# A gated mix of two attention paths: two second feature differences and two low weight parts on POOL in place of VectorE

## The chip, the core and the metric

The kernel runs on one core of a Trainium2 chip. The metric is the device time of one execution in microseconds (us). Five engines work side by side, each through its own queue in order: TensorE (PE in the profile; its weight loads are listed as PEld), VectorE (DVE), ScalarE (ACT), GpSimd (POOL) and SyncE (SP), whose queue in this kernel issues the DMA transfers. They wait for each other through semaphores.

## What is computed

Two attention paths read the same input x of 2048 tokens by 448 features, with 16 heads of 28 features each, and a gate per token mixes them.

```python
def _A_ref(x, wqkv, w_phi, wo):
    qkv = (x @ wqkv) -> q, k, v per head
    pq = jnp.einsum("bhsd,hdf->bhsf", q, w_phi)
    pk = jnp.einsum("bhsd,hdf->bhsf", k, w_phi)
    phi_q = jnp.concatenate([_softmax(pq, axis=-1), _softmax(-pq, axis=-1)], axis=-1)
    phi_k = jnp.concatenate([_softmax(pk, axis=-1), _softmax(-pk, axis=-1)], axis=-1)
    kv = jnp.einsum("bhsf,bhsd->bhfd", phi_k, v)
    z  = jnp.einsum("bhsf->bhf", phi_k)
    num = jnp.einsum("bhqf,bhfd->bhqd", phi_q, kv)
    den = jnp.einsum("bhqf,bhf->bhq", phi_q, z)[..., None] + 1e-6
    return (num / den) -> all heads side by side @ wo

g = _sigmoid((x * gate_w).sum(-1, keepdims=True))
a = _A_ref(x, A_wqkv, A_w_phi, A_wo)
b = softmax attention of x with B_wqkv, B_wo
return g * a + (1 - g) * b
```

Path A is a linear attention whose features are two softmaxes, one of the projected values and one of their negatives. Path B is an ordinary softmax attention over all 2048 keys.

## The kernel before

**Numbers.** Operands of the large matmuls are split in two parts: a high part, which is a copy in TensorE's rounded format, and a low part, the difference between the raw value and the high part. A product then takes three passes (high by high, high by low, low by high). `split_weight` (lines 141 to 144) makes both for a weight: ScalarE copies the high part at once, and the subtraction for the low part is put into a list, `lows`, which `take_lows` (line 137) empties later in the program.

**Stages.** First come the projections of path B's queries and keys, then a loop over i from 0 to 42 (line 694). Its first 16 turns treat path A's key tiles of 128 tokens, turns 16 to 31 the query tiles, with q = i - 16 the number of the tile, and the rest drains what is under way. After that path B's scores, exponentials and value products fill the larger part of the time. Between these, `mx_unit` (line 238) works through the maxima of path B's scores: four small matmuls (pmd and pmb, line 260), two Relu activations (line 264) and two VectorE operations with a running maximum (line 265).

**One query tile in the loop.** In the order of the program text, turn q does this:

1. PE projects the tile into the PSUM tile `pq` (line 729).
2. `features1` (line 420): ScalarE copies pq to SBUF (`pc`, line 423). VectorE reduces the largest and the smallest value of each head (`ext`, lines 425 and 426). POOL subtracts the largest value (the first difference, line 431). The second difference, smallest value minus pc (line 433), is made by the engine that the caller passes. The exponential over both (line 436) is put into the list `exps`.
3. From q = 8 on, and in a few earlier turns, one `mx_unit`.
4. In every second turn from q = 7 on, `normalize2` (line 387) for an earlier pair of tiles: VectorE adds a constant to the denominators `dena` and takes the reciprocal (lines 390 and 391); SyncE stores them to DRAM (`rda`, line 395) and reads them back broadcast to 128 partitions (`rsa`, line 396).
5. From q = 10 on, in every second turn, `normalize4` (line 405): ScalarE makes the high part of a normalized pair and POOL the low part (`oTa`, lines 410 and 411).
6. The exponential of the tile before, q - 1 (line 436, ScalarE).
7. `features2` (line 439) for tile q - 1: VectorE sums (line 443) and takes the reciprocal (line 444), POOL multiplies (line 445).
8. In every second turn from q = 9 on, `normalize3` (line 400): VectorE multiplies a pair by the broadcast `rsa` (line 402).
9. `take_lows` (line 761), then, in turns 4 and 6, `split_part` for a half of woA (lines 770 and 771). Since `take_lows` stands ahead of it, the two low parts of woA come in turns 5 and 7.
10. `numer` in every second turn (line 513): PE makes numerators and denominators (`pn`), ScalarE copies them out (`oUa`, line 381), SyncE moves the denominators (`dena`, line 384).
11. `turn` (line 497): PE transposes the features of an earlier tile (`pft`, line 507), ScalarE copies them (`fT`, line 510).
12. From q = 11 on, `out_a` (line 527): PE multiplies `oTa` by woA, high and low part (`poa`); ScalarE scales by the gate (`ga`, line 535) and SyncE stores it (`gad`).

**PSUM.** pq, pn, pft and poa share four PSUM banks (lines 63 and 718), so a new one waits until the one four places earlier has been copied out by ScalarE. The matmuls of `mx_unit` have four banks of their own.

**Order.** The order of PE, VectorE, ScalarE and POOL is that of the program text (`manual_schedule`, lines 52 to 54). SyncE is not in that list: the order of its transfers is set by the framework when the program is built.

**Staging.** Raw weights of the query stage lie in a pool of two buffers (`stg`, line 713). woA arrives in both (`part_loads`, line 767). The raw weights of path B's values, `wvB`, are loaded into the same two buffers (line 769), each after the low part of woA has been taken from it.

The lines that the change touches stand in this loop: line 735, which names the engine of the second difference for each query tile, and line 771, which splits woA.

Of the kernel before, what the change touches and what calls it, by code (L numbers as in the profile page):

```python
# [19 lines left out]
D = 448  # L20
# [21 lines left out]
def gated_mix_kernel(ctx, tc, xT, wqkB, wvB, wvA, wkAT, wqAT, phi, woA, woB,  # L42
# [7 lines left out]
    nc = tc.nc  # L50
# [90 lines left out]
    def split_weight(w, raw, bs, cs, low=nc.vector, high=nc.scalar.copy):  # L141

        high(w[:, 0, bs, cs], raw)
        lows.append(lambda: low.tensor_sub(w[:, 1, bs, cs], raw, f32(w[:, 0, bs, cs])))
# [20 lines left out]
    def take_acts():  # L165
        while acts:
            acts.pop(0)()

    def take_subs():
        while subs:  # L170
            subs.pop(0)()
# [66 lines left out]
    def mx_unit():  # L238

        u = mxs["u"]  # L240
        if u == NF:
            return
        mx_fin()
        mxs["u"] = u + 1
        gq, r = divmod(u, 16)
        g, qb = divmod(gq, NQ)
        c, qt = divmod(r, 4)
        hp, b = divmod(c, 2)
        col = 64 * gq + 16 * b + 4 * qt + 2 * hp
        if r in (4, 9) and gq + 1 < GM:  # L250
            pair_query(gq + 1, r // 9)
        if r == 4 and gq + 1 == GM:
            mx_query(GM)
        qc, kc = mxs[("qp", gq, hp)], mxs[("kp", g, c)]

        pm = [ps_mx(f"pm{'ddbb'[j]}{u}_{j % 2}") for j in range(4)]
        for j in range(4):
            i = (j + 2) % 4
            js = slice(32 * i, 32 * i + DH)
            nc.tensor.matmul(pm[j], qc[js, qt * P:(qt + 1) * P], kc[js, :], start=True, stop=True,  # L260
                             tile_position=(32 * i, 0))
        for i in range(2):
            rl = rlp.tile([P, 512], F32, tag="rl", name=f"rl{u}_{i}", bufs=psn[2])
            nc.scalar.activation(rl, pm[i], AF.Relu)  # L264
            nc.vector.tensor_tensor_reduce(rl, pm[2 + i], rl, 1.0, LOWEST, ALU.add, ALU.max,  # L265
                                           part[:, col + i:col + i + 1])
        if gq + 1 < GM and qt == 3 and qb == NQ - 1:
            pair_load(g + 1, c)
        if gq + 1 == GM and qt == 3:
            mx_load(GM // NQ, c)  # L270
        if r == 15:
            mx_reduce(gq)
# [147 lines left out]
    def features1(pp, nm, eng):  # L420

        pc = bd.tile([P, H, DH], F32, tag="pc", name=f"pc{nm}", bufs=2)
        nc.scalar.copy(pc, pp[:, :D].rearrange("p (h f) -> p h f", f=DH))
        ext = bd.tile([P, 2, H], F32, tag="ext", name=f"ext{nm}", bufs=3)
        nc.vector.tensor_reduce(ext[:, 0, :], pc, AX.X, ALU.max)
        nc.vector.tensor_reduce(ext[:, 1, :], pc, AX.X, ALU.min)
        fw = bd.tile([P, H, 64], F32, tag="feat", name=f"feat{nm}", bufs=4)
        f = fw[:, :, :2 * DH].rearrange("p h (s f) -> p h s f", s=2)
        if nm in ("k0", "k1", "k2", "k3"):
            nc.gpsimd.memset(fw[:, :, 2 * DH:], 0.0)  # L430
        nc.gpsimd.tensor_sub(f[:, :, 0, :], pc,
                             ext[:, 0, :].unsqueeze(2).to_broadcast([P, H, DH]))
        eng.tensor_sub(f[:, :, 1, :],
                             ext[:, 1, :].unsqueeze(2).to_broadcast([P, H, DH]), pc)
        fe = fw[:, :, :2 * DH]
        exps.append(lambda: nc.scalar.activation(fe, fe, AF.Exp))
        return fw
# [12 lines left out]
    def take_exps(left=0):  # L450
        while len(exps) > left:
            exps.pop(0)()

    fk, va, fq, fT_of, num, oTs = {}, {}, {}, {}, {}, {}
# [26 lines left out]
    def kv_copy():  # L481

        kvT = ta.tile([P, D], F32, tag="ga", name="kvT", bufs=2)
        kvw = kvT[:, :256].rearrange("p (g f) -> p g f", f=64)
        nc.vector.memset(kvw[:, :, 56:], 0.0)
        nc.scalar.copy(kvw[:, :, :56],
                       pkv[:, :224].rearrange("p (g f) -> p g f", f=56))
        return kvT
# [93 lines left out]
    def split_part(w, key, n, i, low=nc.vector):  # L582
        split_weight(w, raws[key][i], slice(2 * i, 2 * i + 2), slice(0, n), low)
# [110 lines left out]
    for i in range(2 * NT + 11):  # L694
        t, q = i, i - NT
        y = q - 1
        tb = y // 2
        take_acts()
        if t < NT and t % 2 == 0:
            mx_unit()  # L700
            passes = (55 if t < NT - 4 else 44) + (4 if t >= 4 else 0)
            pace["n"], pace["at"] = 4 if t >= 4 else 0, [k * passes // 4 for k in range(1, 4)]
        if q in (0, 1):
            take_exps()

        if t % 2 == 0 and 0 <= t - 4 < NT:
            kv_add(t - 4)
            kv_add(t - 3)
        if q == 2:
            bk_s.close()  # L710
            ta_s = ExitStack()
            ta = ta_s.enter_context(tc.tile_pool(name="ta", bufs=1, reuse_waits="tile"))
            stg = ta_s.enter_context(tc.tile_pool(name="stg", bufs=2, reuse_waits="tile"))
            KV = ta.tile([P, 2, P], F32, name="KV")
            kvT = kv_copy()
            ps_s_.close()
            ps = ps_s_.enter_context(tc.tile_pool(name="psq", bufs=1, space=PSUM, reuse_waits="tile"))
            psn[0] = 4
            woA_s = weights(3, "woA_s")
            wvB_s = weights(2, "wvB_s")  # L720
            take_exps()
        if t < NT:
            pk = ps_s(f"pk{t}")
            tok_major(pk, t, wkA_s, D, tick)
            fk[t] = features1(pk, f"k{t}", nc.gpsimd)
            take_exps(1)
        if 0 <= q < NT:
            pq = ps_s(f"pq{q}")
            tok_major(pq, q, wqA_s, D)
        if q == 0:  # L730
            fk[NT - 1] = features2(fk[NT - 1], f"k{NT - 1}")
        if q in (1, 2):
            fq[q - 1] = features2(fq[q - 1], f"q{q - 1}")
        if 0 <= q < NT:
            fq[q] = features1(pq, f"q{q}", nc.vector if q in (1, 3, 4, 5, 6, 7, 8) else nc.gpsimd)
        if 0 <= t - 1 < NT - 1:
            fk[t - 1] = features2(fk[t - 1], f"k{t - 1}")
        if q in (0, 1) or q >= 8:
            mx_unit()
        if y >= 6 and y % 2 == 0 and tb - 3 < 8:  # L740
            num[tb - 3] = normalize2(ta, *num[tb - 3], f"a{tb - 3}", 2, True)
        if y >= 9 and y % 2 and tb - 4 < 8:
            oTs[tb - 4] = normalize4(ta, num.pop(tb - 4), f"a{tb - 4}", 2)
        if q > 0:
            take_exps(int(q < NT))
        if q == 3:
            kv_out(kvT)
        if 2 <= q - 1 < NT:
            fq[q - 1] = features2(fq[q - 1], f"q{q - 1}")
        take_subs()  # L750
        if t == 1:
            pair_load(0, 3)
        if y >= 8 and y % 2 == 0 and tb - 4 < 8:
            num[tb - 4] = normalize3(*num[tb - 4], 2)
        if t < NT:
            value_a(t)
            if t % 2 and t < NT - 4:
                proj_qk(NP + t // 2, ev)
        if q in (0, 1):
            proj_qk(NP + 6 + q, ev)  # L760
        take_lows()
        if 2 <= i < 6:
            fold(wqA_s, "q", i - 2)
        if q == 1:
            ev_s.close()
        if q == 2:
            part_loads("woA", woA, D, "woA")
        if q == 11:
            part_loads("wvB", wvB, D, "wvB")
        if q in (4, 6):  # L770
            split_part(woA_s, "woA", D, (q - 4) // 2)
        if q in (14, 17):
            split_part(wvB_s, "wvB", D, (q - 14) // 3)
        if q == 1:
            gates()
        if y >= 4 and y % 2 == 0 and tb - 2 < 8:
            numer(tb - 2)
        if y < 9 or y % 2:
            if y >= 2 and y - 2 < NT:
                turn(y - 2)  # L780
        if 0 <= y - 10 < NT:
            out_a(y - 10)
            out_a2(y - 10)
        if y >= 9 and y % 2 == 0 and y - 2 < NT:
            turn(y - 2)
        if NT + 3 <= q < NT + 10:
            mx_unit()
        if q == NT + 6:
            ps_s_.close()
            ps = ps_s_.enter_context(tc.tile_pool(name="psv", bufs=1, space=PSUM, reuse_waits="tile"))  # L790
            psn[:2] = 2, 6
        if q == NT + 2:
            bd_s.close()
            vb = [value_tile(0)]
        if 0 <= q - NT - 2 < 8:
            value_b(q - NT - 2)
# [434 lines left out]
```

## Time and profile before

| what | value |
|---|---|
| median of three runs | 985.07 us (985.03 to 985.94) |
| profiled execution, device time | 983.83 us |
| its span, first to last instruction | 982.0 us |
| mean granted TensorE clock | 0.998 of full |
| query stage, turns 0 to 15 | from about 186 us; the last tile's features near 263 us |
| the stretch that the change touches | about 203 to 222 us |

The profile shows one execution. Its page gives the busy time of each engine, a row of the costliest groups of instructions, and the chain of waits followed back from the last instruction. In a row of a group stand the line of the code, the engine, the operation, the tiles written and read, their size and type, the count, the busy time in us and the mean of one in ns, and then the idle time ahead of them with what ended it. Tiles of one name are counted together: featq is the feature tile of a query tile, oUa, oTa, rsa, rda and dena belong to path A's normalization, oUb, oTb, rsb and denb to path B's. A row of the timeline gives the start and the length in us; in brackets stands the idle time of the engine just before, and what ended it. In the chain of waits, "issue" is time in which an engine waited for nothing that the profile shows, and SPq is SyncE's queue.

### The profile page before, as it was taken

How to read it: one execution, taken by the hardware profiler on the slowest of the kernel's cores; microseconds unless marked ns; L12 is line 12 of the kernel's file. 1: busy time of each engine (PE TensorE's matmuls, PEld its weight loads, DVE VectorE, ACT ScalarE, POOL GpSimd, SP SyncE). 2: the span in 40 equal slices, each digit the busy share in tenths (PEclk: the TensorE clock that was granted, in tenths of full speed). 3: DMA queues.
4: the chain of work that ended last, by engine and by line, in shares of the span. 5: the costliest groups of instructions: out<-in, count | busy, mean ns of one | idle time of the engine just before them, and what ended most of it. 6: DMA issues, size and time to landing. Idle time of an engine off the chain costs nothing.

```text
span 982.0 us, 22542 instructions
## 1 busy us (share of the span) xinstructions
PE 973.6 (99%) x8510; PEld 602.8 (61%) x8510; DVE 724.1 (74%) x1335; ACT 752.3 (77%) x1442; POOL 235.9 (24%) x229
## 2 busy tenths in 40 slices
PE   9999999999999999999999999999999999999998
PEld 8877877776877664555555555555555555555555
DVE  5566767898765678888888888888888888885112
ACT  5455655577876688898898898898898898897662
POOL 1135535578744800031011011011011011010010
PEclk9999999999999999999999999999999999999999
DMA  9973010113233233121232121122231222100441
GB/s 307 311 255 113 33 54 32 40 26 92 76 108 120 89 118 123 41 58 41 67 89 69 41 62 41 61 79 68 70 83 41 65 62 65 41 21 31 141 151 57
DMA packets 56140, 84.49 MB, mean 86 GB/s; under 512 B 17216, under 2 KB 23984, under 8 KB 56032
## 3 DMA queue, kind: packets, MB, share of 16 engines
q1 hardware_dynamic: 56032, 83.06, 27.1%
q8 instruction: 67, 1.10, 0.5%
q14 instruction: 41, 0.34, 0.1%
HBM read 54.86 MB, written 27.78 MB: 84 GB/s over the span
## 4 chain that ended last, share of the span: by engine, by line
PE 91%; DVE 4%; DMA 2%; issue 1%; ACT 1%; POOL 0%; SPq 0%; DVEq 0%; POOLq 0%; ACTq 0%
PE g L850 29%; PE pv L995 27%; PE pqk L109 5%; PE pk L127 4%; PE pva L127 4%; PE g L288 3%; PE poa L109 3%; PE pob L109 3%; PE pmd L260 3%; PE pvb L127 2%; PE pvb L109 1%; PE pq L109 1%; PE pqk L621 1%; DMA rsa<-rda 1%; DMA gad<-ga 1%
## 5 line engine op out<-in xcount | busy, mean ns | idle before, releaser
L858 ACT ACTIVATE p<-g 128x512 f32<-128x512 f32 x1020 | 525.6, 609 | 82.8 <-PE g L850 82.6
L295 DVE TENSOR_REDUCE part<-g 128x1 f32<-128x512 f32 x704 | 442.4, 684 | 84.0 <-PE g L288 82.8
L850 PEld LDWEIGHTS g<-qst,kst 32*128 32x128 f32 x3060 | 221.2, 183 | 215.5 <-DVE part L295 194.8
L850 PE MATMUL g<-qst,kst 32*128 32x512 f32 x3060 | 338.0, 419 | 0.1
L995 PE MATMUL pv<-p,vb 128*32 128x512 f32 x2048 | 273.0, 605 | 0.0
L288 PE MATMUL g<-kc,qc 28*128 28x512 f32 x704 | 233.3, 495 | 0.0
L402 POOL TENSOR_TENSOR oUb<-oUb,rsb 128x512 f32<-128x512 f32 x15 | 19.3, 1288 | 491.5 <-DMA rsb<-rdb 369.2
L265 DVE CUSTOM_DVE_ANT_0 rl<-pmb,rl 128x512 f32<-128x512 f32 x160 | 103.3, 683 | 45.5 <-ACT rl L264 45.5
L264 ACT ACTIVATE rl<-pmd 128x512 f32<-128x512 f32 x160 | 87.4, 601 | 32.0 <-PE pmb L260 29.7
L288 PEld LDWEIGHTS g<-kc,qc 28*128 28x128 f32 x704 | 86.3, 181 | 0.2
L995 PEld LDWEIGHTS pv<-p,vb 128*32 128x32 f32 x2048 | 40.6, 108 | 66.0 <-issue 64.7
L109 PE MATMUL pqk<-XH,wB 128*128 128x512 f32 x192 | 59.1, 396 | 0.0
L260 PE MATMUL pmb<-kp,qp 28*128 28x512 f32 x160 | 43.2, 495 | 1.9 <-DVE part L265 1.1
L559 ACT CAST ev<-pqk 128x512 fp32r<-128x512 f32 x28 | 16.0, 589 | 37.8 <-PE pqk L109 21.5
L1006 DVE SCALAR_TENSOR_TENSOR acc<-pob,gate,acc 128x448 f32<-128x448 f32 x12 | 8.2, 684 | 48.3 <-PE pob L109 35.2
L109 PE MATMUL poa<-woA_s,oTa 128*128 128x448 f32 x192 | 43.7, 376 | 0.0
L109 PEld LDWEIGHTS pqk<-XH,wB 128*128 128x128 f32 x192 | 35.4, 188 | 8.5 <-issue 1.5
L560 DVE TENSOR_TENSOR ev<-pqk,ev 128x512 fp32r<-128x512 f32 x28 | 19.0, 690 | 29.3 <-ACT ev L559 29.2
L260 PE MATMUL pmd<-kp,qp 28*128 28x512 f32 x160 | 39.9, 494 | 0.0
L127 PE MATMUL pk<-wkA_s,XH 128*128 128x448 f32 x128 | 39.4, 382 | 0.0
L109 PEld LDWEIGHTS poa<-woA_s,oTa 128*128 128x128 f32 x192 | 34.9, 188 | 6.7 <-issue 3.0
L109 PE MATMUL pq<-wqA_s,XH 128*128 128x448 f32 x128 | 37.4, 374 | 0.6 <-ACT oUa L381 0.6
(156 smaller groups left out, 1073.3 us busy)
## 6 DMA issues: line engine op xcount, KB each, us to landing
qkd<-ev SPq DMA_DIRECT2D x28, 512.0 KB
qst<-qkd SPq DMA_DIRECT2D x64, 112.0 KB
kst<-qkd SPq DMA_DIRECT2D x64, 112.0 KB
od<-oTb SPq DMA_DIRECT2D x48, 112.0 KB
rsa<-rda SPq DMA_DIRECT2D x8, 512.0 KB
oL<-od SPq DMA_DIRECT2D x8, 512.0 KB
rsb<-rdb SPq DMA_DIRECT2D x15, 256.0 KB
gad<-ga SPq DMA_DIRECT2D x16, 224.0 KB
```

Of the source, the lines that this page charges most:

```text
L109: nc.tensor.matmul(dst, l, r, start=i == 0, stop=i == len(todo) - 1)
L127: nc.tensor.matmul(dst[:, :n], l, r, start=i == 0, stop=i == len(todo) - 1, skip_group_check=True)
L260: nc.tensor.matmul(pm[j], qc[js, qt * P:(qt + 1) * P], kc[js, :], start=True, stop=True, tile_position=(32 * i, 0))
L264: nc.scalar.activation(rl, pm[i], AF.Relu)
L265: nc.vector.tensor_tensor_reduce(rl, pm[2 + i], rl, 1.0, LOWEST, ALU.add, ALU.max, part[:, col + i:col + i + 1])
L288: nc.tensor.matmul(pm, mxs[("qc", gq)][js, qt * P:(qt + 1) * P], mxs[("kc", gq // NQ, kb)][js, :], start=True, stop=True, tile_position=(3 ...
L295: nc.vector.tensor_reduce(part[:, col:col + 1], pm, AX.X, ALU.max)
L402: (nc.gpsimd if n == 1 else nc.vector).tensor_mul(oU, oU, rs)
L560: nc.vector.tensor_sub(e[:, 1, :], pq, f32(e[:, 0, :]))
L850: nc.tensor.matmul(st[j], kst_of[(gq // NQ, kt // 4)][js, k, (kt % 4) * P:(kt % 4 + 1) * P], qst_of[gq][js, q, :], start=n == 0, stop=n == ...
L858: nc.scalar.activation(p, st[j], AF.Exp, scale=SCALE)
L995: nc.tensor.matmul(pv[32 * j:32 * j + 32, :], vb[kt // 8][:, kt % 8, 4 * g + j, :], pt[j], start=kt == 0, stop=kt == NT - 1, tile_position ...
```

## The change

```diff
         if 0 <= q < NT:
-            fq[q] = features1(pq, f"q{q}", nc.vector if q in (1, 3, 4, 5, 6, 7, 8) else nc.gpsimd)
+            fq[q] = features1(pq, f"q{q}", nc.vector if q in (1, 3, 5, 7, 8) else nc.gpsimd)
...
         if q in (4, 6):
-            split_part(woA_s, "woA", D, (q - 4) // 2)
+            split_part(woA_s, "woA", D, (q - 4) // 2, nc.gpsimd)
```

The second difference of query tiles 4 and 6 (128 x 448 elements each, fp32) is made by POOL; tiles 1, 3, 5, 7 and 8 stay on VectorE, the others were on POOL already. The low part of woA, in two pieces of 128 x 896 elements, is made by POOL: `split_part` passes the engine on to `split_weight`, where it replaces VectorE as the engine of the subtraction. Both pieces keep their places in the program text, the `take_lows` of turns 5 and 7, behind `features2` of tiles 4 and 6. The high parts stay on ScalarE. What is computed is the same.

## The prediction

> **What bounds the kernel now.** I read the page first, then a table of stretches, then the chain of waits, then the timelines of the engines around the change. The page gives the span and the engines:
>
> ```profile
> span 982.0 us, 22542 instructions
> PE 973.6 (99%) x8510; PEld 602.8 (61%) x8510; DVE 724.1 (74%) x1335; ACT 752.3 (77%) x1442; POOL 235.9 (24%) x229
> ```
>
> TensorE (PE) is idle for 8.4 us in all. The table of stretches (length, busy time of PE, weight loads, VectorE, ScalarE and POOL, then granted clock, DMA share, GB/s) shows that much of it lies in the first third of the query stage, where the change is:
>
> ```profile
> 204.00:210.00 6.00, 5.81 (x63) 4.50 (x62) 5.83 (x9) 4.74 (x10) 4.55 (x5) 1.00 0.03 3
> 221.10:222.60 1.50, 0.44 (x3) 0.13 (x2) 1.28 (x4) 0.53 (x1) 1.50 (x2) 1.00 0.85 265
> 223.60:227.00 3.40, 3.40 (x40) 2.13 (x40) 3.37 (x9) 2.40 (x5) 2.30 (x2) 0.50 0.49 107
> 250.00:260.00 10.00, 10.00 (x60) 8.81 (x59) 7.62 (x17) 7.76 (x15) 7.18 (x7) 1.00 0.21 66
> 290.00:330.00 40.00, 39.94 (x209) 30.47 (x207) 20.31 (x60) 23.98 (x47) 21.57 (x21) 1.00 0.32 105
> ```
>
> VectorE is full from 204 to 210 (5.83 of 6). From 221.1 to 222.6 PE is idle 1.06 of 1.50, and right behind it the granted clock is 0.50 for 3.40 us. Later PE has next to no gap (10.00 of 10, 39.94 of 40), so what is lost or won by about 236 should reach the end one for one. The chain of waits (start, length, what) names what hands over to PE:
>
> ```profile
> 218.87 0.96 DVE woA_s L144
> ...
> 219.84 0.39 SPq L132
> ...
> 220.33 10.05 DMA rsa<-rda
> ...
> 235.83 2.86 PE poa L109 x12
> ```
>
> The chain runs on VectorE, through the second low part of woA, into SyncE's queue and through one broadcast load (rsa, 10.05 us), and ends in PE's work. From the first poa (output of path A) on, PE is in it. So I ask one thing: when does the first poa start, against 235.8 now?
>
> **The change part by part.** Four instructions move, none is added; no DMA is issued more or less. Their prices:
>
> ```profile
> L433 POOL TENSOR_TENSOR featq<-extq,pcq 128x448 f32<-128x448 f32 x9 | 8.5, 944 | 0.0
> L144 POOL TENSOR_TENSOR woB_s<-woB_raw,woB_s 128x448 fp32r<-128x448 f32 x4 | 4.6, 1147 | 0.3
> L411 POOL TENSOR_TENSOR oTb<-oUb,oTb 128x512 fp32r<-128x512 f32 x15 | 19.3, 1285 | 1.2
> L144 DVE TENSOR_TENSOR woA_s<-woA_raw,woA_s 128x896 fp32r<-128x896 f32 x2 | 2.1, 1028 | 0.0
> ```
>
> A second difference costs POOL 0.94 us. A low part of 896 columns on POOL is not in the trace. Two rows have its operands and types: 448 columns take 1147 ns, 512 take 1285, which is 2.16 ns a column; 1285 + 384 x 2.16 = 2114 ns. From above, two parts of 448 are 2.29 us; from below, POOL's product over 896 columns (1.70 us when nothing disturbs it, row below, one operand broadcast) is the nearest. I take 2.1, the row with the same operation; VectorE's price is 1.03.
>
> By the Trainium skill, "GPSIMD Engine Reference", section 4.1 (Engine selection), a two-input elementwise operation belongs on VectorE, GpSimd being about twice as slow; its 4497 ns for 2048 fp32 columns (section 3.1) would make 896 about 1.97 us, an estimate of mine from that page. That speaks against the change as the rows do; by it the sum below would be some 0.2 us smaller.
>
> Now I walk the queues. The timeline (start, length, engine, work, what the wait was for):
>
> ```profile
> 204.00 1.32 POOL L431 TENSOR_TENSOR featq<-pcq,extq 128x448 f32<-128x448 f32 x1
> 205.36 0.95 ACT L436 ACTIVATE featq<-featq 128x896 f32<-128x896 f32 x1
> 206.84 0.67 PE L109 MATMUL pq<-wqA_s,XH 128*128 128x448 f32 x2 [0.19 <-ACT oUa L381]
> 209.54 1.03 DVE L144 TENSOR_TENSOR woA_s<-woA_raw,woA_s 128x896 fp32r<-128x896 f32 x1
> 209.76 2.36 POOL L445 TENSOR_TENSOR featq<-featq,fsumq 128x896 f32<-128x896 f32 x1 [0.73 <-DVE fsumq L444]
> 213.44 0.95 ACT L436 ACTIVATE featq<-featq 128x896 f32<-128x896 f32 x1 [0.38 <-POOL featq L431]
> 214.13 1.70 POOL L445 TENSOR_TENSOR featq<-featq,fsumq 128x896 f32<-128x896 f32 x1 [0.72 <-DVE fsumq L444]
> 214.92 0.67 PE L109 MATMUL pq<-wqA_s,XH 128*128 128x448 f32 x2 [0.43 <-ACT oUa L381]
> 215.09 1.22 DVE L433 TENSOR_TENSOR featq<-extq,pcq 128x448 f32<-128x448 f32 x1
> 219.01 2.36 POOL L445 TENSOR_TENSOR featq<-featq,fsumq 128x896 f32<-128x896 f32 x1 [1.90 <-ACT rl L264]
> 221.87 0.68 DVE L265 CUSTOM_DVE_ANT_0 rl<-pmb,rl 128x512 f32<-128x512 f32 x1
> 222.61 1.11 PE L260 MATMUL pmb<-kp,qp 28*128 28x512 f32 x2 [1.07 <-DVE part L265]
> 230.47 1.51 DVE L402 TENSOR_TENSOR oUa<-oUa,rsa 128x1024 f32<-128x1024 f32 x1 [1.42 <-DMA rsa<-rda]
> ```
>
> VectorE and POOL exclude each other in these two-input operations. POOL's product takes 1.70 us by itself, but 2.36 behind the low part that ends at 210.57: 1.55 us after that. VectorE's difference at 215.09 ends 0.48 us after the product that ends at 215.83. I use this below.
>
> Tile 4's difference leaves VectorE and follows the first one on POOL, which, no longer disturbed, takes 0.94: 204.00 + 0.90 + 0.94 = 205.84. The exponential of tile 4 waits for it: 205.87 against 205.36, 0.5 later. Behind it on ScalarE stand the copies that free the PSUM bank for pq of tile 6, so PE starts that at 207.36 against 206.84.
>
> First low part: on POOL it stands behind the product of tile 4 (209.5 to 211.2, now undisturbed) and ends near 213.3. Behind it stand both differences of tile 6: the second ends at 213.22 + 0.90 + 0.94 = 215.06. The exponential of tile 6 then starts at 215.09 against 213.44 (+1.65), and through the same copies pq of tile 8 at 216.6 against 214.92. VectorE is relieved of a second difference (1.22 us in the row of tile 7) and a low part (1.03) by then, and of another difference in tile 6, but spends it waiting: pq of tile 6 comes 0.5 later and POOL holds the lock, so that the reciprocal for the broadcast is ready near 217.5, where SyncE sends it on now (217.57, below).
>
> Second low part: behind the product of tile 6 (219.04 to 220.74) POOL holds it from 220.70 to 222.80. VectorE's difference of tile 8 waits for the lock until then, so the maxima L265 start at 223.2 instead of 221.87 and PE's pmb at 223.96 instead of 222.61.
>
> SyncE is the third queue, and here I choose. Its timeline:
>
> ```profile
> 210.59 0.41 SPq L132 DMA_DIRECT2D wvB_raw<-in_wvB_dram  x1
> 217.57 1.18 SPq L395 DMA_DIRECT2D rda<-dena  x2
> 218.84 0.57 SPq L384 DMA_DIRECT2D dena<-oUa  x1
> 219.84 0.39 SPq L132 DMA_DIRECT2D wvB_raw<-in_wvB_dram  x1
> 220.33 0.54 SPq L396 DMA_DIRECT2D rsa<-rda  x1
> 223.75 1.62 SPq L176 DMA_DIRECT2D qp<-qkd  x4
> 227.75 1.10 SPq L395 DMA_DIRECT2D rda<-dena  x2
> 231.87 0.53 SPq L396 DMA_DIRECT2D rsa<-rda  x1
> ```
>
> Each part of wvB is loaded into the buffer that a low part of woA has read last: 0.01 to 0.02 us behind the ends at 210.57 and 219.83. The second stands ahead of rsa, with four qp loads and the next rda behind. If the order stays, the wvB load goes out at 222.82 and rsa at 223.31, 2.98 us later than now, and lands at 233.36. VectorE starts L402 at 233.45 against 230.47. It gets 0.3 back there, as the product of tile 8 on POOL is over (1.51 becomes 1.16); then come the extremes of tile 10, POOL's two differences and L411, and the first poa starts **2.7 us later**. The losses above lie under this wait.
>
> PE then has a hole of about 3 us before pmb (233.1 to 236.3). A hole of 1.1 to 1.2 us cost a stretch of 3.40 us at clock 0.50 above, at most 1.7 us of work. Here part of the stretch falls into the wait for L411: I add 0.5, bounds 0 and 1.7.
>
> By the Trainium skill, "TensorE: Matmul & The Clock Gate", section "HAM oscillation — how this bites in real kernels", only idle gaps above about 3.4 us should be avoided; by it the term is 0 and the sum 2.7. The row above disagrees: about 1.2 us was enough here, so I keep the term.
>
> Sum: 2.7 + 0.5 = +3.2 us. Against the profiled execution (983.83 us, span 982.0 and 1.83 around it) that is 987.0. The median of the three runs, 985.07, is 1.24 above it, so I predict 985.07 + 3.2 = **988.3 us**. With 1.7 us for a low part VectorE's difference of tile 8 takes the lock first and the part ends at 223.3 all the same (+3.2); with 2.0 to 2.3 the wait is 2.6 to 3.1. With the clock's bounds the case runs from +2.6 to +4.9, 987.7 to 990.0.
>
> **Rivals.** *rsa goes out first.* SyncE's order is not written out by hand, as those of the other four engines are; the row order is that in which transfers become ready. rsa needs its rda landed, at the latest 220.3 now; the wvB part would be ready only at 222.8. If they change places, rsa is issued by 220.3 and lands by 230.4. VectorE gets to L402 1.35 later than now, but there it now idles 1.42 for rsa: 1.35 - 1.42 and 0.2 behind it on POOL make +0.1, with 2.3 us for a low part +0.5, with 1.7 -1.4. Time 985.2, 983.7 to 986.0. For it speaks the readiness, against it only that the order of the profile is what I have.
>
> *POOL is cheap (the other side).* If a low part cost POOL what it costs VectorE, 1.03 us, and rsa went first, the lock at tile 8 would be gone, VectorE would be 0.7 us ahead and would not idle 1.42 for rsa: -2.1, 983.0 us. The sign turns at about 2.05 us for a low part, and beyond -0.2% it comes only near 1.1. For it speaks the full VectorE (5.83 of 6), against it that 448 columns alone took 1147 ns.
>
> *POOL's queue and the clock together.* rsa first, but PE's holes before tile 8 and at pmb (1.4 and 1.0 us) both bring slow stretches: the delays of 1.7 and 1.35 then stay and up to 1.7 us more comes on top, some +2.5, 987.6. Against it: VectorE and POOL, not PE, set the poa in that case.
>
> **How the numbers follow.** Order kept, +3.2: 0.50. rsa first, +0.1: 0.30. POOL cheap, -2.1: 0.10. Holes and clock: 0.05. The last 0.05 is for a loss under 0.2% that I have no mechanism for. The bound of 0.2% (1.97 us) is about what a measurement of this kernel can tell from no change. Slower 0.50 + 0.05 = 0.55, same 0.30 + 0.05 = 0.35, faster 0.10. The range for 8 in 10 takes in the first two cases without the cheap end of the second and the dear end of the first: 984.4 to 989.7; the likeliest case's own is 987.7 to 990.0.
>
> **What would show it.** Right: two POOL rows at L144 for woA of about 2.1 us, one ahead of tile 6's differences and one ending near 222.8; the exponential of tile 6 waiting for POOL's L433; SyncE issuing the second wvB part at about 222.8 with rsa behind it; L402 waiting over 3 us for rsa; a second stretch of low clock or a moved one. The forecast is wrong if rsa stands ahead of the second wvB part, if the low parts take under 1.7 us, or if PE shows gaps after 250 that take up the shift.

## The result and the profile after

The changed kernel takes 989.16 us, median of 16 runs (987.1 to 991.99), beside 985.01 for the kernel before, median of 16 runs on the same chips. The ratio is 1.0035, 95% interval 1.0024 to 1.0046: 3.4 us slower, between 2.4 and 4.5 (the two medians lie 4.15 us apart; the ratio is what the text relies on). Forecast were 988.3 us and +3.2.

The profiled execution took 989.8 us. Its page has these lines for the span and the engines:

```profile
span 988.0 us, 22540 instructions
PE 975.1 (99%) x8510; PEld 603.3 (61%) x8510; DVE 723.9 (73%) x1331; ACT 752.3 (76%) x1442; POOL 238.6 (24%) x233
```

PE is busy 1.5 us longer, and the span is 6.0 us longer, so most of the loss is idle time of PE. The four moved instructions show in the counts of VectorE (1335 to 1331) and POOL (229 to 233).

Before the two executions are compared, one thing has to be taken off. The changed one is late already where nothing was changed. First its row, then that of the kernel before, at the start of the program:

```profile
4.80 3.06 PE L621 MATMUL pqk<-XH,wB 128*128 128x512 f32 x8
...
202.10 1.06 PE L507 MATMUL pft<-ident,featq 128*128 128x128 f32 x8 [0.81 <-ACT fT L510]
```

```profile
4.79 2.22 PE L621 MATMUL pqk<-XH,wB 128*128 128x512 f32 x8
...
201.31 1.06 PE L507 MATMUL pft<-ident,featq 128*128 128x128 f32 x8 [0.81 <-ACT fT L510]
```

Eight matmuls at the start took 3.06 us instead of 2.22, and the same transposes ahead of the change come 0.79 us later. The code there is the same in all ten kernels of this text, and in their profiled executions this row takes from 2.08 to 3.06 us: it differs from execution to execution. Below, "net" means that a difference of start times has these 0.79 us taken off. The net loss of this execution is then 5.2 us of span, more than the 3.45 by the ratio; the section on the prediction returns to that.

The chain of waits of the changed kernel (start, length, what) runs through the same places as before, with POOL in VectorE's place:

```profile
219.75 1.70 POOL featq L445
...
221.45 1.92 POOL woA_s L144
...
223.39 0.39 SPq L132
...
223.87 10.53 DMA rsa<-rda
...
237.46 1.40 PE pmb L260 x2
238.86 1.89 PE pn L520 x32
240.75 3.42 PE poa L109 x12
```

The second low part is POOL's, SyncE's load of wvB follows it, the broadcast load rsa follows that. Behind VectorE's share of it come the same three steps of PE as before, and each is longer. In the chain of the kernel before two of them read (the third, poa, stands in the prediction with 2.86):

```profile
234.31 0.49 PE pmb L260
234.80 1.02 PE pn L520 x32
```

SyncE's queue, from the timeline of the changed kernel:

```profile
218.30 1.18 SPq L395 DMA_DIRECT2D rda<-dena  x2
...
223.39 0.39 SPq L132 DMA_DIRECT2D wvB_raw<-in_wvB_dram  x1
223.87 0.54 SPq L396 DMA_DIRECT2D rsa<-rda  x1
```

The order is that of before. The store rda leaves at 218.30 against 217.57, net nothing. Then, after one more small transfer (dena at 219.57), the queue stands still until POOL has read the buffer, and rsa leaves 5.57 us behind rda, where it was 2.76.

The engines around it, from the timeline of the changed kernel:

```profile
208.15 0.68 PE L109 MATMUL pq<-wqA_s,XH 128*128 128x448 f32 x2 [0.71 <-ACT oUa L381]
211.97 1.95 POOL L144 TENSOR_TENSOR woA_s<-woA_raw,woA_s 128x896 fp32r<-128x896 f32 x1
215.75 0.95 ACT L436 ACTIVATE featq<-featq 128x896 f32<-128x896 f32 x1 [1.37 <-POOL featq L433]
217.23 0.67 PE L109 MATMUL pq<-wqA_s,XH 128*128 128x448 f32 x2 [1.43 <-ACT oUa L381]
221.41 1.95 POOL L144 TENSOR_TENSOR woA_s<-woA_raw,woA_s 128x896 fp32r<-128x896 f32 x1
221.58 2.26 DVE L433 TENSOR_TENSOR featq<-extq,pcq 128x448 f32<-128x448 f32 x1
224.51 1.10 PE L260 MATMUL pmb<-kp,qp 28*128 28x512 f32 x2 [0.66 <-DVE part L265]
234.52 1.23 DVE L402 TENSOR_TENSOR oUa<-oUa,rsa 128x1024 f32<-128x1024 f32 x1 [3.56 <-DMA rsa<-rda]
237.46 1.40 PE L260 MATMUL pmb<-kp,qp 28*128 28x512 f32 x2 [3.46 <-DVE part L265]
240.68 3.49 PE L109 MATMUL poa<-woA_s,oTa 128*128 128x448 f32 x12
```

A low part takes POOL 1.95 us. The exponential of tile 6 waits for POOL's second difference, and PE's pq of tile 8 comes 1.52 net later. VectorE's difference at 221.58 is held until the low part ends at 223.36. VectorE then waits 3.56 us for rsa, and PE 3.46 us for VectorE's maxima behind that.

The table of stretches of the changed kernel (columns as in the prediction):

```profile
228.00:235.00 7.00, 6.01 (x35) 4.60 (x33) 3.37 (x9) 2.30 (x5) 3.80 (x4) 1.00 0.30 82
235.00:242.00 7.00, 4.54 (x38) 2.42 (x39) 6.96 (x16) 6.18 (x11) 5.65 (x5) 0.54 0.20 63
250.00:260.00 10.00, 10.00 (x82) 8.30 (x81) 6.99 (x15) 7.12 (x13) 7.87 (x7) 1.00 0.17 53
290.00:330.00 40.00, 39.89 (x205) 30.39 (x204) 20.82 (x59) 23.64 (x46) 16.00 (x13) 1.00 0.32 101
```

Between 228 and 235 VectorE is busy 3.37 of 7 us: it waits for rsa. Between 235 and 242 PE is idle 2.46 us and runs at a granted clock of 0.54. From 250 on PE is full, as before, so nothing of the loss is won back.

### The profile page after: what moved, and what is told of

Same layout as the page of the kernel before. It is cut to its first block, busy times and chain, and to the rows that moved or that the text cites. A ratio compares the mean times of both kernels' runs of the same rounds, so it can differ in the third digit from the quotient of the medians.

```text
span 988.0 us, 22540 instructions
## 1 busy us (share of the span) xinstructions
PE 975.1 (99%) x8510; PEld 603.3 (61%) x8510; DVE 723.9 (73%) x1331; ACT 752.3 (76%) x1442; POOL 238.6 (24%) x233
## 4 chain that ended last, share of the span: by engine, by line
PE 90%; DMA 3%; DVE 2%; issue 1%; POOL 1%; ACT 1%; SPq 0%; DVEq 0%; POOLq 0%; ACTq 0%
PE g L850 29%; PE pv L995 26%; PE pqk L109 5%; PE pk L127 4%; PE pva L127 4%; PE g L288 3%; PE poa L109 3%; PE pob L109 3%; PE pmd L260 3%; PE pvb L127 2%; PE pq L109 2%; PE pvb L109 1%; PE pqk L621 1%; DMA rsa<-rda 1%; DMA gad<-ga 1%
## 5 line engine op out<-in xcount | busy, mean ns | idle before, releaser
L402 POOL TENSOR_TENSOR oUb<-oUb,rsb 128x512 f32<-128x512 f32 x15 | 19.3, 1285 | 491.3 <-DMA rsb<-rdb 356.8
```

Of the source, the lines that this page charges most:

```text
L402: (nc.gpsimd if n == 1 else nc.vector).tensor_mul(oU, oU, rs)
```

## The experiments

The theory is that of the forecast: the loss is the second wvB load, which waits in SyncE's queue for POOL's second low part and holds rsa behind it. The rivals are that the loss comes from POOL's queue and the lock between VectorE and POOL (late exponentials, late maxima), or from the low clock alone. The medians, each against the kernel before on the same chips (985.01 us for the changed kernel, 985.09 for e2 to e5, 985.08 for e1 and e6 to e8):

| kernel | on POOL | rsa ahead of the second wvB load | us (runs) | ratio, 95% interval |
|---|---|---|---|---|
| changed kernel | differences, both low parts | no | 989.16 (16) | 1.0035 (1.0024 to 1.0046) |
| e5_after_rsa | differences, both low parts | yes | 985.82 (12) | 1.0008 (0.9996 to 1.0020) |
| e3_second | second low part | no | 989.37 (6) | 1.0041 (1.0025 to 1.0056) |
| e7_second_rsa | second low part | yes | 985.73 (11) | 0.9997 (0.9985 to 1.0008) |
| e1_lows | both low parts | no | 988.39 (12) | 1.0031 (1.0019 to 1.0042) |
| e4_first | first low part | no | 985.75 (12) | 1.0003 (0.9994 to 1.0013) |
| e2_diffs | differences | no | 985.87 (12) | 1.0006 (0.9997 to 1.0015) |
| e6_before_rsa | none | yes | 985.67 (12) | 0.9997 (0.9985 to 1.0009) |
| e8_diffs_second_rsa | differences, second low part | yes | 985.05 (11) | 0.9993 (0.9980 to 1.0006) |

**The changed kernel with two transfers exchanged.** Only SyncE's order differs from the changed kernel: the second part of wvB is to be issued behind the first pair's rsa.

```diff
+    rs_ins = []
+    def behind(ins, fn):
+        with tc.issue_after(ins):
+            return fn()
...
-        nc.sync.dma_start(rs.rearrange("p n q -> p (n q)"),
-                          rd.unsqueeze(1).to_broadcast([4, 32, n * 512]))
+        rs_ins.append(nc.sync.dma_start(rs.rearrange("p n q -> p (n q)"),
+                          rd.unsqueeze(1).to_broadcast([4, 32, n * 512])))
...
-            part_loads("wvB", wvB, D, "wvB")
+            loads("wvB", lambda: load_part(wvB, D, "wvB", 0), lambda: behind(rs_ins[0].ins, lambda: load_part(wvB, D, "wvB", 2)))
```

> The changed kernel with two transfers exchanged in SyncE's queue: the broadcast load rsa of the first pair of tiles ahead of the second wvB part. Queue theory (the loss is rsa standing behind a wvB load that waits for POOL's second low part): rsa goes out near 220.5 instead of 223.9 and lands before VectorE asks for it; no wait of L402, no stretch of clock 0.50 near 236 to 242; within 1 us of before, 984 to 986. Rival, POOL theory (POOL's longer queue ahead of tiles 6 and 8 delays PE and the clock by itself): the holes ahead of tile 8 and at pmb remain and the time stays at 987 or more.

Measured 985.82 us. SyncE's and VectorE's rows from its timeline, and then a row of its list of waits (what PE waited for between 203 and 240 us, total, times, longest):

```profile
217.68 1.18 SPq L395 DMA_DIRECT2D rda<-dena  x2
...
220.30 0.53 SPq L396 DMA_DIRECT2D rsa<-rda  x1
222.76 0.39 SPq L132 DMA_DIRECT2D wvB_raw<-in_wvB_dram  x1
...
231.06 2.20 DVE L402 TENSOR_TENSOR oUa<-oUa,rsa 128x1024 f32<-128x1024 f32 x1 [0.73 <-DMA qp<-qkd]
```

```profile
PE pq L109 <- ACT oUa L381: 2.2, 2, 1.4
```

rsa leaves 2.62 us behind rda, and VectorE's wait falls from 3.56 to 0.73 us. POOL's low parts stay, and so does the late pq (1.4 us of wait, as in the changed kernel); still the median falls by 3.3 us (2.7 by the ratios, whose intervals do not overlap), and what is left cannot be told from none. The loss was the place of one transfer in SyncE's queue. Two signs that were expected did not come: rsa still lands after VectorE asks for it (by the chain of waits 10.64 us after 220.30, at 230.94; the bracket names qp, which the profile puts last), and a stretch of low clock is left behind PE's next wait (its row stands in the section on the prediction).

**Which of the four instructions does it.** Each of these two is the kernel before with one low part on POOL.

```diff
-            split_part(woA_s, "woA", D, (q - 4) // 2)
+            split_part(woA_s, "woA", D, (q - 4) // 2, nc.gpsimd if q == 6 else nc.vector)
```

> The kernel before with the second low part of woA alone on POOL. Queue theory: this one instruction carries nearly the whole loss, +2.9 us of wait for rsa and the slow stretch of the clock behind it, 988 to 989.5. POOL theory: one instruction in a queue with room (no second differences of tiles 4 and 6 on it) costs next to nothing, 985.

```diff
-            split_part(woA_s, "woA", D, (q - 4) // 2)
+            split_part(woA_s, "woA", D, (q - 4) // 2, nc.gpsimd if q == 4 else nc.vector)
```

> The kernel before with the first low part of woA alone on POOL. Queue theory: no transfer of weight waits behind it; 984.5 to 985.5 although tile 6 comes about 1.2 us later (the wait of 1.42 us for rsa covers it). POOL theory: POOL holds up tile 6's exponential and PE's tile 8, 986 or more.

The second low part alone costs all of it, 989.37 us; the first alone gives 985.75, no difference that can be told. That median lies between the two expectations, and its interval, up to 1.3 us, does not shut out the 0.9 us of the POOL theory. The timeline of the kernel with the second alone:

```profile
221.23 2.32 POOL L144 TENSOR_TENSOR woA_s<-woA_raw,woA_s 128x896 fp32r<-128x896 f32 x1
...
223.58 0.39 SPq L132 DMA_DIRECT2D wvB_raw<-in_wvB_dram  x1
224.07 0.54 SPq L396 DMA_DIRECT2D rsa<-rda  x1
...
233.18 1.23 DVE L402 TENSOR_TENSOR oUa<-oUa,rsa 128x1024 f32<-128x1024 f32 x1 [4.31 <-DMA rsa<-rda]
236.12 1.40 PE L260 MATMUL pmb<-kp,qp 28*128 28x512 f32 x2 [3.53 <-DVE part L265]
```

The picture of the changed kernel is there with a single instruction moved: the load of wvB right behind POOL's end, rsa behind the load, VectorE idle 4.31 us, PE 3.53, and a mean granted clock of 0.57 from 234 to 242.

**The two differences alone.** The list of line 735 as in the changed kernel, both low parts on VectorE.

> The kernel before with the two second differences (tiles 4 and 6) alone on POOL. Queue theory: 984.5 to 985, about -0.5 us, since VectorE writes the reciprocals a little earlier and rsa goes out earlier; POOL theory: PE starts tile 6 0.5 us later and keeps the delay, 985.5 to 986.

Measured 985.87 us. The small gain expected did not come, and the median lies in the range of the POOL theory; its interval, -0.3 to 1.5 us, tells neither a gain nor a loss. In the profiled execution the step that was to bring the gain is there:

```profile
217.28 1.18 SPq L395 DMA_DIRECT2D rda<-dena  x2
...
233.33 1.40 PE L260 MATMUL pmb<-kp,qp 28*128 28x512 f32 x2 [1.59 <-DVE part L265]
```

rda leaves 0.49 us earlier than before (its transposes start at 201.51, so 0.20 us are taken off), and rsa with it. But PE waits 1.59 us there, the granted clock is 0.60 on average from 234 to 242, and the first poa starts at 236.55, 0.59 us later than before. Whether the other executions lost the gain in this way is not shown.

**Both low parts, without the differences.**

```diff
-            split_part(woA_s, "woA", D, (q - 4) // 2)
+            split_part(woA_s, "woA", D, (q - 4) // 2, nc.gpsimd)
```

> Both low parts on POOL, the differences as before, SyncE's order as before. Queue theory: the second part brings its wait, +2.1 us and the slow stretch, 987.5 to 989.5, no more than with the second part alone. POOL theory: more than with the second part alone, since both parts are in POOL's queue, 989.5 to 991.

Measured 988.39 us. The interval overlaps those of the changed kernel and of the second low part alone: no addition by the first low part or by the differences can be told. The 989.5 us or more that the POOL theory gave are 4.4 above the kernel before, outside the interval, which ends at 4.1.

**The exchange without the loss, three times.** The exchange of the first experiment in the kernel before, in the kernel with the second low part alone, and in that with the two differences besides.

> The kernel before with rsa of the first pair ahead of the second wvB part, nothing else. If the wvB part takes bandwidth from rsa, rsa lands in about 7.5 to 8 us in place of 10.05, L402 no longer waits 1.42 us, and the time falls by up to 1.3 us, 983.7 to 984.5. If rsa's 10 us are its own, 985.

> The second low part alone on POOL, with rsa ahead of the second wvB part. Queue theory: the loss of the same kernel without the exchange (+4 us) is gone wholly, and VectorE, relieved of 0.94 us, is ahead: 983 to 984.5. POOL theory: some loss stays, 985.5 or more.

> Both second differences and the second low part on POOL, the first low part on VectorE, rsa ahead of the second wvB part: every piece moved but the one ahead of tile 6. Queue theory: about -2 us, 982.5 to 984. POOL theory: as the changed kernel without its wait, 985.5 to 986.5.

The exchange takes the whole loss from the second low part (989.37 to 985.73 us): this is the cleanest pair, with no other difference in the kernel, though the two were measured on different chips, each beside the kernel before. The gains expected beyond that are misses in all three: 985.67, 985.73 and 985.05 us are the kernel before within the intervals. The second of them lies in the range that the POOL theory gave, a range that reaches into its interval, so it speaks for neither. Why the exchange alone wins nothing shows in SyncE's rows of the kernel before with it:

```profile
217.53 1.18 SPq L395 DMA_DIRECT2D rda<-dena  x2
...
220.16 0.53 SPq L396 DMA_DIRECT2D rsa<-rda  x1
220.74 0.47 SPq L132 DMA_DIRECT2D wvB_raw<-in_wvB_dram  x1
...
229.95 1.99 DVE L402 TENSOR_TENSOR oUa<-oUa,rsa 128x1024 f32<-128x1024 f32 x1 [0.94 <-DMA qp<-qkd]
```

With nothing ahead of it rsa still leaves 2.63 us behind rda, against 2.76 in the kernel before: it needs rda landed (in the chain of waits of the first experiment rda lands at 218.32 + 1.92 = 220.24, and rsa leaves at 220.30). So the wvB load's place in the queue held rsa for 0.13 us only. What rsa would take without the wvB load beside it is not shown, since that load still follows 0.58 us behind. In the kernel with the exchange and the second low part alone VectorE still waits:

```profile
218.76 1.18 SPq L395 DMA_DIRECT2D rda<-dena  x2
...
221.38 0.53 SPq L396 DMA_DIRECT2D rsa<-rda  x1
...
230.61 1.83 DVE L402 TENSOR_TENSOR oUa<-oUa,rsa 128x1024 f32<-128x1024 f32 x1 [1.10 <-DMA rsa<-rda]
```

2.62 us again, then about 9 us of transfer, and VectorE idle 1.10 us at the end of it. The second low part stands behind the reciprocals in VectorE's order, so taking it away cannot send rda or rsa earlier; the time that VectorE saves there goes into the wait for rsa. No version tried is measurably faster than the kernel before.

## Why the prediction was right

**The place and the mechanism** were as forecast: SyncE keeps its order, the second wvB load waits for POOL, rsa waits behind it, VectorE waits for rsa, and PE waits for VectorE. Not one of these was left to the argument alone: the exchange of two transfers removes the loss twice (changed kernel, 3.3 us; second low part alone, 3.6 us), and moving that one instruction brings it. The choice on which the forecast hung, that SyncE keeps its order, had a chance of 0.50 beside 0.30 for the other order, and spoke only from the order seen in the profile; nothing else that the forecast had could decide it. To that extent the hit is also luck.

**A low part on POOL** was put at 2.11 us and took 1.95 in the changed kernel, 2.32 in the kernel with the second alone. The slope between the two narrow rows was too steep to carry on: from 1285 ns for 512 columns to 1950 ns for 896 is 1.73 ns a column, not 2.16. The estimate from the Trainium skill, "GPSIMD Engine Reference", section 3.1, was 1.97 us; the trace agrees with that one better than with mine.

**The delay of rsa** was forecast at 2.98 us and is 223.87 - 220.33 - 0.79 = 2.75 net; the 0.16 us less for the low part explains most of the difference. L402 starts 3.26 later (234.52 - 230.47 - 0.79), since rsa itself took 10.53 us instead of 10.05, and lost 0.28 in length as forecast (1.51 to 1.23). The net delay at its end is 2.98 us, where the sum had 2.7.

**The smaller losses under it** came close: pq of tile 6 0.52 later (forecast 0.5), the exponential of tile 6 1.52 (1.65), pq of tile 8 1.52 (1.7), pmb of tile 8 224.51 - 222.61 - 0.79 = 1.11 (1.35). They lie under the wait, as the sum had it: with them in place and the wait gone, 985.82 us is left.

**The clock** is the mis-sized term in the profiled execution. From the end of L402 to the end of the first poa block the net delay grows from 2.98 to 240.68 + 3.49 - 235.76 - 2.93 - 0.79 = 4.69 us: 1.7 us more at a clock of 0.54, the upper bound of 0 to 1.7, where 0.5 was added. That bound came from the stretch of 3.40 us in the kernel before; 7 us at a mean of 0.54 are some 6.4 us at 0.50, an estimate from the row above, so 1.7 was no bound for this stretch. 1.43 us of it stand in the two chains: pn took 1.89 us instead of 1.02, poa 3.42 instead of 2.86. The medians don't ask for so much: of their 3.45 us (by the ratio), 2.98 are the wait, if it is the same in every execution, and 0.5 are left, with an interval of -0.6 to 1.6. The mean granted clocks of the 16 executions fit a term that some pay and others don't. Seven have 0.998, as the profiled execution of the kernel before has, and took 987.1 to 988.5 us, median 987.9, which is 2.9 above the median of the kernel before: about the wait alone. Nine have 0.995 to 0.997 and took 988.4 to 992.0, median 990.15, which is 5.1 above. A mean over the whole execution doesn't say where the clock was low, so this is a fit and not a proof; by it the 0.5 is an average of about nothing and about 2.

Where the low clock follows a gap of PE could not be settled either. By the Trainium skill, "TensorE: Matmul & The Clock Gate", section "HAM oscillation — how this bites in real kernels", gaps above about 3.4 us are the ones to avoid. The 3.46 us of the changed kernel agree in length, though the clock was down before that time had passed: PE is idle from 234.00, and the granted clock is 1.00 from 234 to 235, 0.80 from 235 to 236 and 0.50 from there. The kernel with the first low part alone agrees with the rule too: its PE waited 1.27 us ahead of a stretch at full clock (its timeline and its table of stretches):

```profile
235.11 1.11 PE L260 MATMUL pmb<-kp,qp 28*128 28x512 f32 x2 [1.27 <-DVE part L265]
```

```profile
234.00:242.00 8.00, 6.77 (x60) 5.10 (x61) 7.90 (x18) 7.19 (x14) 7.89 (x8) 1.00 0.23 70
```

Against the rule stand the kernel before, with 0.50 behind 1.06 us of idle time, and the changed kernel with the two transfers exchanged:

```profile
234.98 1.11 PE L260 MATMUL pmb<-kp,qp 28*128 28x512 f32 x2 [1.59 <-DVE part L265]
```

```profile
234.00:242.00 8.00, 6.89 (x55) 5.31 (x55) 7.90 (x18) 6.12 (x12) 7.90 (x8) 0.79 0.21 70
```

Its gap of 1.59 us is followed by a mean clock of 0.79. So gaps of 1.1 to 1.6 us bring the low clock in some executions and not in others, and the term could only be given as bounds.

**The rivals.** *rsa goes out first* fell with SyncE's order, which is the same in both kernels although rsa was ready earlier than the load. Its time was right for the kernel in which the order is changed by hand: 985.2 forecast, 985.82 measured, with an interval of -0.4 to +2.0 us around the kernel before. *POOL is cheap* needed a low part near 1.1 us; it takes 1.95. *POOL's queue and the clock together*, +2.5 us with rsa first, lies outside that interval; the profiled execution of that kernel shows the gap and the low clock, and at 986.98 us it lies 1.2 above the median of its kernel.

**Three figures of the forecast** don't follow from what it shows, and none changes its sum. The gap of PE in the kernel before is 1.06 to 1.07 us, not 1.1 to 1.2. By the figure of the Trainium skill, 1.97 us, the sum would be 2.11 - 1.97 = 0.14 us smaller, not 0.2. The upper end of the second case, +0.5, is 985.6 us, not 986.0.

## What to carry to other kernels

An instruction that reads a staging buffer last also gives the time at which the next load into that buffer can leave, and in a queue that issues in order it gives the time of everything behind that load. Before moving such an instruction to a slower engine, read the queue of the transfers behind it: here 2 us more on POOL cost nothing that could be told once that load was out of the way, and 3.4 us with it in the way, because a 10 us broadcast load stood behind a load that nobody needed yet. In these kernels relief of the busy VectorE brought nothing that could be told, as it still had to wait for that transfer.

## What the hardware showed beside that

VectorE's addition to 32 columns (line 390) takes much longer while POOL works on a product. The row of this line in the kernel before gives the shortest, median and longest of its eight executions in ns; below it stand two rows from the timeline of the changed kernel:

```profile
L390 DVE TENSOR_SCALAR dena<-dena x8: 175/475/916, 216.2 to 298.5; 128x32 f32<-128x32 f32 x8
```

```profile
215.68 2.16 POOL L445 TENSOR_TENSOR featq<-featq,fsumq 128x896 f32<-128x896 f32 x1
216.21 1.68 DVE L390 TENSOR_SCALAR dena<-dena 128x32 f32<-128x32 f32 x1
```

At 175 ns when least disturbed, it takes 1.68 us here: it starts inside POOL's product and ends at 217.89, just behind the product's end at 217.84. This small operation with one tile as input is held as the larger ones are; the forecast had counted the lock for the two-input operations only. It does not go for every operation with one input: VectorE's sum (line 443) at 208.70 keeps its 1.07 us beside POOL's L431, which runs from 208.25 to 209.57.
